# Linear attention and a sine MLP on one core: first hidden blocks by batch pairs, first k through two queues, decay moved from q to x, order redrawn

## The chip, the cores and the metric

The kernel runs on one core of a Trainium2 chip. The metric is device time of one execution in microseconds (us); lower is better. Engines are named as in the profile: PE is TensorE (PEld its weight loads), DVE is VectorE, ACT is ScalarE, POOL is GpSimd, SP is SyncE.

## The reference

Attention with decay, block by block, then an MLP with a sine. B = 4 batches, H = 8 heads, S = 768, D = 64; 3072 tokens, d_model 512, d_ff 2048, all fp32.

```python
for b in range(nb):                                   # causal blocks of the sequence
    intra = einsum('bhic,bhjc->bhij', qb, kb) * Dmask # lam^(i-j) for i >= j, else 0
    intra = einsum('bhij,bhjd->bhid', intra, vb)
    inter = einsum('bhid,bhde->bhie', qb * lam_pow, kv_state)   # lam^(i+1)
    out[:, :, sl] = intra + inter
    kv_state = lam_block * kv_state + einsum('bhsd,bhse->bhde', kb * rev_pow, vb)
x = out.transpose(0, 2, 1, 3).reshape(B * S, H * D)
h = x @ w_in
g = h + sin(alpha * h) ** 2 / (alpha + 1e-09)
y = g @ w_out
```

## The kernel before

The sequence is cut into six blocks t of T = 128 positions; a group g = t is that block of all four batches, 512 tokens. For each t the kernel forms scores transposed (`scores`, L241: k turned times q turned, heads in four row groups of 32, 32 products of 128 columns for a pair pr of batches), multiplies them on VectorE by a table of decays (`mask`, L253), adds the part that comes from the carried state (`carried`, L288) and the part inside the block (`inside`, L298) in four PSUM banks, one for each a (two heads), and casts them to xt in bf16 (`leave`, L312, a copy on ScalarE). The state is updated by `states` and `new_state` (L266, L277). The table C0 of t > 0 holds only the factor of k; the factor of q, lam^(i+1), is multiplied into the raw q on GpSimd by `scale_raw` (L261, word z) before `turn` (L232) transposes it on VectorE.

For each group the MLP has 16 blocks f of 128 hidden units: `hidden` (L321, four products of 512 columns), `sine` (L327, ScalarE), `square` (L331: on ScalarE for q, on VectorE as scalar_tensor_tensor for P, as tensor_tensor for Q), and `finish` (L341, VectorE, s^2 * r + h into gall). Then `project` (L347) multiplies gall by w_out in four parts of four f for each of four batches m, and `store` (L355) copies the result on ScalarE and sends it from SP. The last one goes in halves (L361).

PSUM has eight banks, which scores, outputs, states, hidden blocks and projections share; a word that needs a bank waits until its last reader is done. Each engine takes its instructions in the order in which the program issues them. From L498 that order is the ORDER table: a word is a step with its indices and, behind the colon, its banks. h, s, q/P/Q, t, u, o, e are the MLP as above; F, m, K, S, O, x are scores, masks, state products, new state, outputs, casts to xt; j and k turn q and k; d multiplies k by its decay on GpSimd (L257); B and C cast the state on ScalarE and GpSimd; r, R, n, v, I, W issue the loads of raw k, raw q, k, v, w_in, w_out from GpSimd's queue, which cast fp32 to bf16 on the way. Such a load waits for the eighth one before it.

The first block, t = 0, is written out ahead of the table (L148 to L460). SP loads k of two batches in fp32 (L150), which VectorE casts (L412); GpSimd loads the other pair (L160). ScalarE makes lnlam (L198) and the masks' table C1 (`decays`, L215), which GpSimd cuts to its triangle (`cut`, L219). k is turned on TensorE (`turn_k0`, L377), q on VectorE. Then follow scores and masks for each pair of batches, the products inside the block (`inside0`, L390) and the casts to xt (`leave0`, L400); `spin` (L182) issues products of ones whose result nobody reads. The last things ahead of ORDER are a `warm` sine on ScalarE (L458), which brings the table of sines, the reciprocal of alpha (L459) and C0 (L224). ORDER begins with h0.0.

Of the kernel before, what the change touches and what calls it, by code (L numbers as in the profile page):

```python
# [8 lines left out]
ALU = mybir.AluOpType  # L9
# [19 lines left out]
m2.1.3 B1.1 B2.0 m2.1.2 u1.1.3 o1.1 z3.0 v3 m2.1.1 z3.1 k3.0 o1.0 u1.2.1 O2:3275 x2.0 x2.1 x2.2 u1.2.2 x2.3 j3.0
F3.0:6043 m3.0.0 u1.2.3 o1.2 h2.0:6 m3.0.2 s2.0 q2.0 m3.0.1 j3.1 h2.1:7 s2.1 q2.1 k3.1 d3.1 h2.5:5 t2.0 R4  # L30
# [27 lines left out]
def kernel(  # L58
# [90 lines left out]
    for b in range(2):  # L149
        nc.sync.dma_start(out=raw_k0[:, b], in_=k[b, :, 0:T, :].rearrange("h p e -> p h e"))  # L150
# [161 lines left out]
    def leave(t, a):  # L312
        A.copy(out=xt[t][:, a, :].rearrange("p (b i) -> p b i", b=B), in_=att["O"][a])  # L313
# [217 lines left out]
```

## Time and profile before

| | us |
|---|---|
| median of 3 runs | 210.99 |
| the runs | 209.92, 210.99, 212.38 |
| profiled execution, its time | 209.95 |
| profiled execution, its span (first to last instruction) | 208.2 |
| busy in it: PE, DVE, ACT, POOL | 194.9, 145.8, 136.2, 100.7 |
| casts to xt on ACT (L313), 20 | 10.4 |
| raw q times decay on POOL (L263), 10 | 19.1 |
| squares on ACT (L335) 64, DVE P (L339) 19, DVE Q (L337) 13 | 39.2, 15.1, 5.5 |

The span counts from the first instruction to the last; the execution's own time has 1.75 us more. Each engine's instructions are dated in us from the start of the span. A product's record covers its pipeline, so that records of one stream overlap; the distance between starts is what one costs. What an engine waited for stands in brackets behind the first instruction after the wait.

### The profile page before, as it was taken

The numbers are of one execution on the slowest core, as the hardware profiler recorded it, in microseconds if no ns is written. First come the engines' busy times: TensorE is split into PE (matmuls) and PEld (weight loads), VectorE is DVE, ScalarE is ACT, GpSimd is POOL, SyncE is SP. The second block draws the span as 40 slices with busy tenths as digits, with TensorE's granted clock in tenths as the row PEclk, the third lists the DMA queues.
The fourth block names the chain that finished last, engine by engine and source line by source line (L and its number), as shares of the span: only waits on it lengthen the run. The fifth ranks groups of instructions, "written<-read, shape, count | busy, mean of one in ns | idle before, by whom it ended". The sixth has DMA issues, their size and how long they took to land.

```text
span 208.2 us, 4876 instructions
## 1 busy us (share of the span) xinstructions
PE 194.9 (94%) x2005; PEld 97.7 (47%) x2032; DVE 145.8 (70%) x218; ACT 136.2 (65%) x241; POOL 100.7 (48%) x116
## 2 busy tenths in 40 slices
PE   6479999999999999899999999999999999999993
PEld 3353444464444454354544564454444444444462
DVE  3486799742999879998897798774637876754300
ACT  4767999027999857948977577965626765455131
POOL 8999847979999986995717380000000000000000
DMA  7999999999995999999709969100111011011042
GB/s 132 166 181 180 187 200 207 170 175 232 213 140 58 153 173 186 122 119 168 49 3 122 180 85 74 50 3 3 50 50 50 0 50 54 0 52 50 4 153 98
DMA packets 65880, 22.61 MB, mean 109 GB/s; under 512 B 46770, under 2 KB 62914, under 8 KB 65858
## 3 DMA queue, kind: packets, MB, share of 16 engines
q0 software_dynamic: 60144, 15.47, 77.1%
q1 hardware_dynamic: 5680, 6.82, 9.4%
q8 instruction: 16, 0.26, 0.5%
q14 instruction: 6, 0.05, 0.1%
q10 hardware_dynamic: 34, 0.01, 0.0%
HBM read 31.47 MB, written 6.29 MB: 181 GB/s over the span
## 4 chain that ended last, share of the span: by engine, by line
PE 67%; POOL 12%; DMA 10%; DVE 4%; issue 4%; ACT 2%; POOLq 0%; DVEq 0%; ACTq 0%
PE ops L351 30%; PE hps L324 28%; DMA w_in<-in_moe_w_in_dram 4%; DMA raw_k<-in_k_dram 3%; DMA nat_v<-in_v_dram 3%; POOL w_in L141 3%; PE F_ps L248 2%; PE O_ps L303 2%; POOL raw_q L263 2%; POOL raw_q L124 2%; POOL nat_v L131 2%; PE ops L366 2%; DVE STm L254 1%; DVE s L339 1%; PE O_ps L294 1%
## 5 line engine op out<-in xcount | busy, mean ns | idle before, releaser
L324 PE MATMUL hps<-xt,w_in 128*128 128x512 bf16 x371 | 89.6, 383 | 1.0 <-issue 0.4
L351 PE MATMUL ops<-w_out,gall 128*128 128x512 bf16 x354 | 84.3, 379 | 1.6 <-issue 1.3
L329 ACT ACTIVATE s_sb<-hps,alpha_sb 128x512 bf16<-128x512 f32 x96 | 63.4, 690 | 27.9 <-PE hps L324 26.1
L344 DVE SCALAR_TENSOR_TENSOR gall<-s,r_sb,hps 128x512 bf16<-128x512 bf16 x96 | 67.7, 737 | 9.2 <-ACT s L335 8.2
L324 PEld LDWEIGHTS <-w_in 128*128 128x128 bf16 x384 | 37.3, 99 | 45.3 <-issue 2.1
L351 PEld LDWEIGHTS <-gall 128*128 128x128 bf16 x368 | 35.0, 98 | 41.7
L335 ACT ACTIVATE s<-s_sb 128x512 bf16<-128x512 bf16 x64 | 39.2, 636 | 1.0
L254 DVE TENSOR_TENSOR STm<-F_ps,C 128x512 bf16<-128x512 f32 x48 | 30.1, 682 | 6.5 <-PE F_ps L248 6.4
L357 ACT COPY o_sb<-ops 128x512 f32<-128x512 f32 x23 | 13.2, 585 | 26.6 <-PE ops L351 25.1
L259 POOL TENSOR_TENSOR nat_k<-nat_k,R 128x1024 bf16<-128x1024 bf16 x10 | 19.1, 1914 | 5.5 <-DMA nat_k<-in_k_dram 5.4
L263 POOL TENSOR_TENSOR raw_q<-raw_q,Rraw 128x1024 bf16<-128x1024 bf16 x10 | 19.1, 1919 | 4.8 <-DMA raw_q<-in_q_dram 4.8
L339 DVE SCALAR_TENSOR_TENSOR s<-s_sb 128x512 bf16<-128x512 bf16 x19 | 15.1, 804 | 7.4 <-ACT s_sb L329 7.2
L238 DVE STREAM_TRANSPOSE turned_q<-raw_q 128x512 f32<-128x512 f32 x12 | 13.0, 1096 | 7.5 <-POOL raw_q L263 5.2
L124 POOL DMA_DIRECT2D raw_q<-in_q_dram x24 | 14.2, 602 | 2.4 <-DVE turned_q L238 1.1
L124 POOL DMA_DIRECT2D raw_k<-in_k_dram x20 | 11.7, 602 | 5.5 <-DVE turned_k L238 4.6
L131 POOL DMA_DIRECT2D nat_v<-in_v_dram x12 | 14.2, 1186 | 0.0
L248 PE MATMUL F_ps<-turned_q,turned_k 32*128 32x128 bf16 x384 | 8.9, 229 | 5.2 <-DVE turned_q L238 2.8
L313 ACT CAST xt<-O_ps 128x512 bf16<-128x512 f32 x20 | 10.4, 596 | 4.7 <-PE O_ps L303 4.6
L337 DVE TENSOR_TENSOR s<-s_sb 128x512 bf16<-128x512 bf16 x13 | 5.5, 423 | 10.7 <-ACT s_sb L329 10.7
L238 DVE STREAM_TRANSPOSE turned_k<-raw_k 128x512 f32<-128x512 f32 x10 | 11.0, 1095 | 1.8 <-DMA raw_k<-in_k_dram 1.8
L248 PEld LDWEIGHTS <-turned_k 32*128 32x128 bf16 x384 | 6.5, 99 | 10.3 <-issue 6.4
L131 POOL DMA_DIRECT2D nat_k<-in_k_dram x9 | 10.7, 1192 | 0.1
(59 smaller groups left out, 86.8 us busy)
## 6 DMA issues: line engine op xcount, KB each, us to landing
out_dram<-o_sb SPq DMA_DIRECT2D x23, 256.0 KB, 2.3
raw_q<-in_q_dram POOLq DMA_DIRECT2D x24, 128.0 KB, 4.6
nat_v<-in_v_dram POOLq DMA_DIRECT2D x12, 256.0 KB, 6.4
raw_k<-in_k_dram POOLq DMA_DIRECT2D x20, 128.0 KB, 5.4
nat_k<-in_k_dram POOLq DMA_DIRECT2D x9, 256.0 KB, 8.5
w_out<-in_moe_w_out_dram POOLq DMA_DIRECT2D x4, 512.0 KB, 10.0
w_in<-in_moe_w_in_dram POOLq DMA_DIRECT2D x6, 256.0 KB, 7.1
raw_k<-in_k_dram SPq DMA_DIRECT2D x2, 256.0 KB, 3.6
```

The source lines that it names most:

```text
L124: (eng or G).dma_start(out=dst[quad[a], bs].rearrange("t b n r d -> t (b n) (r d)"), in_=src[t, a])
L131: G.dma_start(out=nat[nm, t][:, bs].rearrange("p b h e -> p (b h) e"), in_=SRC[nm][bs, :, t * T:(t + 1) * T, :].rearrange("b h p e -> p (b ...
L238: V.transpose(out=dst.rearrange("p (x t r) -> p x r t", r=R, t=32), in_=src.rearrange("p (x r d) -> p x r d", r=R, d=32))
L248: nc.tensor.matmul(out=F[a][:, u, n, :], lhsT=kt[:, :, e] if t else kt[:, e, :], rhs=KQ["q", t][quad[a], 2 * pr + u, n, :, e], start=(e == ...
L254: V.tensor_tensor(out=st[t, pr][:, a], in0=att["F", pr][a], in1=(C0 if t else C1)[:, a].unsqueeze(1).broadcast_to([P, 2, NQ, T]), op=ALU.mult)
L259: G.tensor_tensor(out=kd, in0=kd, in1=R128[:].unsqueeze(1).unsqueeze(3).broadcast_to([P, 2, H, D]), op=ALU.mult)
L263: G.tensor_tensor(out=qs, in0=qs, in1=Rraw[:].rearrange("p n r -> p (n r)").unsqueeze(1).unsqueeze(3).broadcast_to([P, 2, NQ * R, D]), op= ...
L324: nc.tensor.matmul(out=hps[g, f][:], lhsT=w_in_sb[f // 4][:, c, (f % 4) * P:(f % 4 + 1) * P], rhs=xt[g][:, c, :], start=(c == 0), stop=(c ...
L329: A.activation(out=s_of[g, f][:], in_=hps[g, f][:], func=ACTF.Sin, scale=alpha_sb[:, f:f + 1])
L335: A.activation(out=s2_of[g, f][:], in_=s_sb[:], func=ACTF.Square)
L344: V.scalar_tensor_tensor(out=gall[g][:, f, :], in0=s2_of.pop((g, f))[:], scalar=r_sb[:, f:f + 1], in1=hps.pop((g, f))[:], op0=ALU.mult, op ...
L351: nc.tensor.matmul(out=ops[g, m][:], lhsT=gall[g][:, f, m * P:(m + 1) * P], rhs=w_out_sb[part][:, f % 4, :], start=(f == 0), stop=(f == NF ...
```

## The change

For t = 0: all four batches of k come in fp32, two from SP and two from ScalarE's queue (alpha's load stands between the latter), and VectorE casts four. GpSimd issues the loads of q first, then makes `dist`, then loads v and the first half of w_in's first quarter; the quarter's other half and the second quarter are issued between the cuts of C1. The hidden blocks f = 0 to 3 of group 0 leave ORDER: `hidden_half` multiplies them by the 256 columns of one pair of batches and one c at a time, between the products inside the block, with more `spin` products among them. Scores of both pairs are issued ahead of all `inside0`. For t > 0: q is no longer scaled (the words z, `scale_raw`, `Rraw` and `ptab` go), and xt gets the factor lam^(i+1) as it leaves PSUM, by a tensor_tensor with the table `Etab` on VectorE in place of the copy on ScalarE. `Etab` is made by four Exp on ScalarE just ahead of the `warm` sine, from `pos_row` and four more columns of lnlam, for which `lam_half` is turned by four more products.

ORDER is redrawn: 651 words for 666. It has the same steps but for the 10 z, the four h and one I (w_in's second quarter); squares are 60 q, 19 P, 17 Q (before 64, 19, 13). The diff, with the table cut to its start:

```diff
--- before.py
+++ after.py
@@ -14,43 +14,42 @@
 ORDER = """
-h0.0:1 s0.0 I1 h0.1:2 s0.1 P0.0 q0.1 t0.0 t0.1 I2 d0.1 h0.2:0 s0.2 h0.3:3 I3 s0.3 q0.2 q0.3 h0.4:6 t0.2 r1 t0.3
-d0.0 h0.5:1 s0.4 s0.5 h0.6:7 P0.4 h0.7:4 s0.6 s0.7 P0.5 t0.4 t0.5 W0 R1 h0.8:5 q0.6 t0.6 s0.8 q0.7 P0.8 W1
...
+s0.0 s0.1 d0.1 P0.0 P0.1 t0.0 t0.1 s0.2 q0.2 t0.2 s0.3 q0.3 t0.3 I2 h0.5:5 h0.4:4 s0.4 s0.5 h0.6:7 h0.7:0 P0.4
+t0.4 q0.5 t0.5 h0.8:2 s0.6 P0.6 t0.6 h0.11:1 h0.9:3 R1 j1.0 I3 s0.7 s0.8 q0.7 t0.7 s0.9 q0.8 t0.8 W0 h0.10:4
+h0.13:6 q0.9 h0.12:7 W1 t0.9 s0.10 h0.14:2 u0.2.0:0 s0.11 h0.15:3 r1 q0.10 P0.11 t0.11 s0.12 s0.13 q0.12 q0.13
+W2 t0.10 j1.1 u0.0.0:1 v1 d0.0 t0.12 s0.14 u0.3.0:4 u0.0.1 K0:57 W3 s0.15 q0.14 t0.13 t0.14 q0.15 t0.15 S0.0
+C0.0 u0.2.1 k1.0 u0.3.1 S0.1 k1.1 F1.0:3527 m1.0.0 m1.0.1 u0.0.2 C0.1 u0.3.2 m1.0.2 m1.0.3 F1.1:6532 m1.1.1
+m1.1.3 u0.1.0:7 u0.2.2 m1.1.2 u0.1.1 m1.1.0 O1:3625 x1.0 x1.3 x1.1 u0.2.3 o0.2 u0.3.3 o0.3 u0.0.3 o0.0 x1.2
+h1.0:5 s1.0 r2 k2.1 k2.0 R2 n1 n2 v2 q1.0 h1.1:1 s1.1 h1.3:3 t1.0 j2.0 q1.1 t1.1 h1.2:4 s1.2 q1.2 t1.2 h1.4:0
...
@@ -145,21 +144,27 @@
-    raw_k0 = gbp.tile([P, 2, H, D], FP32, name="raw_k0", tag="gall")
-    for b in range(2):
-        nc.sync.dma_start(out=raw_k0[:, b], in_=k[b, :, 0:T, :].rearrange("h p e -> p h e"))
+    raw_k0 = gbp.tile([P, B, H, D], FP32, name="raw_k0", tag="gall")
     alpha_fp = consts.tile([NFC, P], FP32, name="alpha_fp")
+
+    def load_k0(eng, b):
+        eng.dma_start(out=raw_k0[:, b], in_=k[b, :, 0:T, :].rearrange("h p e -> p h e"))
+
+    load_k0(nc.sync, 0)
+    load_k0(A, 1)
+    load_k0(nc.sync, 2)
     A.dma_start(out=alpha_fp[:], in_=moe_alpha.rearrange("(f p) -> f p", p=P))
-    dist = consts.tile([P, T], FP32, name="dist")
-    G.iota(out=dist[:], pattern=[[1, T]], base=0, channel_multiplier=-1, allow_small_or_imprecise_dtypes=True)
+    load_k0(A, 3)
     new_raw(0, "q")
     new_nat(0, "k")
     new_nat(0, "v")
     for a in range(NA):
         load_raw(0, "q", a)
-    load_nat(0, "k", 1)
+    dist = consts.tile([P, T], FP32, name="dist")
+    G.iota(out=dist[:], pattern=[[1, T]], base=0, channel_multiplier=-1, allow_small_or_imprecise_dtypes=True)
     load_nat(0, "v", 0)
     load_nat(0, "v", 1)
+    load_w_in(0, 2, 0)
     fill = consts.tile([P, 512], BF16, name="fill")
     V.memset(fill[:], 1.0)
     one = consts.tile([1, 1], FP32, name="one")
@@ -168,10 +173,6 @@
     delta = consts.tile([P, T], FP32, name="delta")
     tri = consts.tile([P, T], FP32, name="tri")
     idf = consts.tile([NFC, NFC], FP32, name="idf")
-    V.tensor_scalar(out=iden[:], in0=dist[:], scalar1=0.0, scalar2=None, op0=ALU.is_equal)
-    V.tensor_copy(out=idf[:], in_=iden[0:NFC, 0:NFC])
-    V.tensor_scalar(out=delta[:], in0=dist[:], scalar1=0.0, scalar2=None, op0=ALU.max)
-    V.tensor_scalar(out=tri[:], in0=dist[:], scalar1=0.0, scalar2=None, op0=ALU.is_ge)
     pcol = consts.tile([P, 2], FP32, name="pcol")
 
     def token_column(n, base, step):
@@ -185,8 +186,8 @@
             nc.tensor.matmul(out=ps[:], lhsT=fill[:, 0:P], rhs=fill[:], start=True, stop=True)
 
     spin(3, 3)
-    lnall = consts.tile([P, H + NQ], FP32, name="lnlam")
-    lnlam, ln_q = lnall[:, 0:H], lnall[:, H:H + NQ]
+    lnall = consts.tile([P, H + NQ + NA], FP32, name="lnlam")
+    lnlam, ln_q, ln_a = lnall[:, 0:H], lnall[:, H:H + NQ], lnall[:, H + NQ:]
     lam_ps = bank("lam_ps", 2)
     for h in range(H):
         nc.tensor.transpose(out=lam_ps[:, h:h + 1], in_=lam_row[:, h:h + 1].broadcast_to([1, P]), identity=one[:])
@@ -195,7 +196,16 @@
     for n in range(NQ):
         nc.tensor.transpose(out=lam_ps[:, H + n:H + n + 1], in_=lam_quad[:].rearrange("p h i -> p (h i)")[
             :, n * P:n * P + P], identity=one[:])
-    A.activation(out=lnall[:], in_=lam_ps[:, 0:H + NQ], func=ACTF.Ln)
+    lam_half = consts.tile([1, NA, NQ, D], FP32, name="lam_half")
+    V.tensor_copy(out=lam_half[:], in_=lam_row[:].rearrange("p (n a) -> p a n", a=NA).unsqueeze(3).broadcast_to([1, NA, NQ, D]))
+    V.tensor_scalar(out=iden[:], in0=dist[:], scalar1=0.0, scalar2=None, op0=ALU.is_equal)
+    V.tensor_copy(out=idf[:], in_=iden[0:NFC, 0:NFC])
+    V.tensor_scalar(out=delta[:], in0=dist[:], scalar1=0.0, scalar2=None, op0=ALU.max)
+    V.tensor_scalar(out=tri[:], in0=dist[:], scalar1=0.0, scalar2=None, op0=ALU.is_ge)
+    for a in range(NA):
+        nc.tensor.transpose(out=lam_ps[:, H + NQ + a:H + NQ + a + 1], in_=lam_half[:, a].rearrange("p n d -> p (n d)"),
+                            identity=one[:])
+    A.activation(out=lnall[:], in_=lam_ps[:, 0:H + NQ + NA], func=ACTF.Ln)
     a_ps = bank("a_ps", 5)
     nc.tensor.transpose(out=a_ps[:, 0:NFC], in_=alpha_fp[:], identity=idf[:])
     spin(2, 3)
@@ -204,8 +214,8 @@
     NE = consts.tile([P, H], FP32, name="NE")
     R128 = consts.tile([P, H], FP32, name="R128")
     L128 = consts.tile([P, NQ], FP32, name="L128")
-    Rraw = consts.tile([P, NQ, R], FP32, name="Rraw")
-    ptab = consts.tile([P, R], FP32, name="ptab")
+    Etab = consts.tile([P, NA, T], FP32, name="Etab")
+    pos_row = consts.tile([P, T], FP32, name="pos_row")
     alpha_sb = consts.tile([P, NFC], FP32, name="alpha_sb")
     r_sb = consts.tile([P, NFC], FP32, name="r_sb")
 
@@ -258,11 +268,6 @@
         kd = nat["k", t][:, 2 * pr:2 * pr + 2]
         G.tensor_tensor(out=kd, in0=kd, in1=R128[:].unsqueeze(1).unsqueeze(3).broadcast_to([P, 2, H, D]), op=ALU.mult)
 
-    def scale_raw(t, pr):
-        qs = raw["q", t][:, 2 * pr:2 * pr + 2].rearrange("p b n r d -> p b (n r) d")
-        G.tensor_tensor(out=qs, in0=qs, in1=Rraw[:].rearrange("p n r -> p (n r)").unsqueeze(1).unsqueeze(3).broadcast_to(
-            [P, 2, NQ * R, D]), op=ALU.mult)
-
     def states(t, bks):
         KV = [bank("KV_ps", n)[:].rearrange("p (b e d) -> p b e d", b=B, e=2) for n in bks]
         kd = nat["k", t][:].rearrange("p b h (d e) -> p b h d e", e=2)
@@ -310,7 +315,8 @@
         inside(t, 1)
 
     def leave(t, a):
-        A.copy(out=xt[t][:, a, :].rearrange("p (b i) -> p b i", b=B), in_=att["O"][a])
+        V.tensor_tensor(out=xt[t][:, a, :].rearrange("p (b i) -> p b i", b=B), in0=att["O"][a],
+                        in1=Etab[:, a].unsqueeze(1).broadcast_to([P, B, T]), op=ALU.mult)
 
     def new_xt(t):
         xt[t] = xtp.tile([P, NDC, GRP], BF16, name="xt")
@@ -405,55 +411,82 @@
         else:
             V.tensor_copy(out=x, in_=o)
 
+    FIRST = (3, 0, 1, 2)
+
+    def hidden_half(pr, *pieces):
+        cols = slice(2 * pr * T, 2 * pr * T + 2 * T)
+        for f, c in pieces:
+            if (0, f) not in hps:
+                hps[0, f] = bank("hps", FIRST[f])
+            nc.tensor.matmul(out=hps[0, f][:, cols], lhsT=w_in_sb[0][:, c, f * P:(f + 1) * P], rhs=xt[0][:, c, cols],
+                             start=(c == 0), stop=(c == NDC - 1), skip_group_check=True)
+
     new_xt(0)
-    decays(0)
-    decays(1)
-    for b in range(2):
+    for b in range(B):
         V.tensor_copy(out=nat["k", 0][:, b], in_=raw_k0[:, b])
     turn(0, "q", 0)
     turn(0, "q", 1)
+    decays(0)
     turn_k0((0,), 4, A)
     turn_k0((1,), 7, A)
+    decays(1)
+    A.copy(out=alpha_sb[:], in_=a_ps[:, 0:NFC])
+    turn_k0((2,), 6, A)
+    turn_k0((3,), 5, A)
     decays(2)
     decays(3)
-    A.copy(out=alpha_sb[:], in_=a_ps[:, 0:NFC])
     cut(0)
     cut(1)
-    load_w_in(0, 2, 0)
+    load_w_in(0, 2, 1)
+    load_w_in(1)
     cut(2)
     cut(3)
-    load_w_in(0, 2, 1)
     token_column(0, -1, -1)
     token_column(1, T - 1, -1)
-    for a in range(NA):
-        G.iota(out=ptab[quad[a]], pattern=[[1, R]], base=1, channel_multiplier=R, allow_small_or_imprecise_dtypes=True)
+    G.iota(out=pos_row[:], pattern=[[1, T]], base=1, channel_multiplier=0, allow_small_or_imprecise_dtypes=True)
+    spin(2, 3)
     scores(0, 0, (0, 1, 2, 3))
-    turn_k0((2, 3), 6, A)
-    for a in range(NA):
-        mask(0, 0, a)
+    spin(1, 4)
+    scores(0, 1, (4, 5, 6, 7))
+    for pr in range(2):
+        for a in range(NA):
+            mask(0, pr, a)
     power(NE, 0)
     power(R128, 1)
+
+    spin(2, 0)
+    ps = open0(0)
+    inside0(0, 0, ps, 0, True)
+    spin(1, 1)
+    inside0(0, 1, ps, 1, False)
+    leave0(0, 0, 2, ps, A)
+    spin(1, 1)
+    ps = open0(1)
+    inside0(0, 2, ps, 0, True)
+    leave0(0, 2, 1, ps, A)
     A.activation(out=L128[:], in_=ln_q, func=ACTF.Exp, scale=float(T))
-    for n in range(NQ):
-        A.activation(out=Rraw[:, n, :], in_=ptab[:], func=ACTF.Exp, scale=ln_q[:, n:n + 1])
-    scores(0, 1, (4, 5, 6, 7))
-    for j in range(2):
-        ps = open0(j)
-        for a in (2 * j, 2 * j + 1):
-            inside0(0, a, ps, a % 2, a % 2 == 0)
-        leave0(0, 2 * j, 2, ps, A)
+    hidden_half(0, (1, 0), (1, 1))
+    ps = open0(2)
+    inside0(0, 3, ps, 0, True)
+    leave0(0, 3, 1, ps, A)
+    hidden_half(0, (0, 0), (0, 1), (0, 2), (1, 2))
+    late = [open0(4), open0(5), open0(6)]
+    inside0(1, 0, late[0], 0, True)
+    hidden_half(0, (0, 3), (1, 3))
+    inside0(1, 1, late[0], 1, False)
+    leave0(1, 0, 2, late[0], A)
+    hidden_half(0, (2, 0), (2, 1), (2, 2), (2, 3))
+    inside0(1, 2, late[1], 0, True)
+    leave0(1, 2, 1, late[1], A)
+    hidden_half(0, (3, 0), (3, 1), (3, 2), (3, 3))
+    hidden_half(1, (0, 0), (0, 1))
+    inside0(1, 3, late[2], 0, True)
+    leave0(1, 3, 1, late[2], V)
+    hidden_half(1, *((f, c) for f in (1, 2, 3) for c in (0, 1)))
+    hidden_half(1, *((f, 2) for f in range(4)))
+    hidden_half(1, *((f, 3) for f in range(4)))
     for a in range(NA):
-        mask(0, 1, a)
-    ps = open0(2)
-    inside0(1, 0, ps, 0, True)
-    inside0(1, 1, ps, 1, False)
-    leave0(1, 0, 2, ps, A)
-    ps = open0(3)
-    inside0(1, 2, ps, 0, True)
-    leave0(1, 2, 1, ps, A)
-    ps = open0(4)
-    inside0(1, 3, ps, 0, True)
-    leave0(1, 3, 1, ps, V)
+        A.activation(out=Etab[:, a, :], in_=pos_row[:], func=ACTF.Exp, scale=ln_a[:, a:a + 1])
     warm = consts.tile([P, 1], FP32, name="warm")
     A.activation(out=warm[:], in_=lnlam[:, 0:1], func=ACTF.Sin)
     V.reciprocal(out=r_sb[:], in_=alpha_sb[:])
@@ -486,7 +519,7 @@
 
     STEP = {
         "I": load_w_in, "W": load_w_out, "r": lambda t: load_raws(t, "k"), "R": lambda t: load_raws(t, "q"),
-        "v": lambda t: load_nats(t, "v"), "n": lambda t: load_nats(t, "k"), "z": scale_raw, "d": decay_k,
+        "v": lambda t: load_nats(t, "v"), "n": lambda t: load_nats(t, "k"), "d": decay_k,
         "k": lambda t, pr: turn(t, "k", pr), "j": lambda t, pr: turn(t, "q", pr), "F": scores_of, "m": mask,
         "K": states_of, "S": new_state, "O": outputs_of, "x": leave_x,
         "B": lambda t, n: cast_state(t, n, A), "C": lambda t, n: cast_state(t, n, G),
```

64 lines of the change are left out of this document (29 added, 35 removed).

## Prediction

> **What bounds the kernel now.** Four views, in this order: busy times by stage, the timeline of the first 20 us, TensorE's weight loads there, TensorE's waits from 60 to 110 us.
>
> ```profile
> 16.00:26.00 10.00, 9.78 (x42) 4.25 (x43) 7.15 (x12) 8.65 (x16) 9.00 (x13) 1.00 1.24 183
> 36.00:46.00 10.00, 9.79 (x176) 5.02 (x178) 6.96 (x11) 1.07 (x2) 8.89 (x13) 1.00 1.61 172
> 86.00:96.00 10.00, 8.63 (x128) 4.28 (x129) 9.78 (x15) 6.65 (x12) 9.99 (x10) 1.00 1.38 127
> ```
> Columns: stretch, length, busy PE, PEld, DVE, ACT, POOL, clock, DMA. From 16 us on PE is nearly always busy; it lacks 1.37 us at 86-96, where DVE is full. The head, and those holes, are all there is to win.
>
> ```profile
> 8.04 2.02 DVE L238 STREAM_TRANSPOSE turned_q<-raw_q 128x512 f32<-128x512 f32 x2 [2.33 <-DMA raw_q<-in_q_dram]
> 9.20 1.04 PE L248 MATMUL F_ps<-turned_q,turned_k 32*128 32x128 bf16 x32 [2.78 <-DVE turned_q L238]
> 10.31 2.48 DVE L254 TENSOR_TENSOR STm<-F_ps,C 128x512 bf16<-128x512 f32 x4 [0.25 <-PE F_ps L248]
> 13.38 2.48 DVE L254 TENSOR_TENSOR STm<-F_ps,C 128x512 bf16<-128x512 f32 x4 [0.58 <-PE F_ps L248]
> 16.17 1.28 ACT L458 ACT_TABLE_LOAD   x1
> 18.25 0.69 ACT L329 ACTIVATE s_sb<-hps,alpha_sb 128x512 bf16<-128x512 f32 x1 [0.59 <-PE hps L324]
> ```
> The head is a chain: q lands (8.04), scores, eight masks (end 15.86), xt, ACT's table of sines, the first hidden block and first sine (18.25).
>
> ```profile
> 16.67 0.15 PEld L324 LDWEIGHTS <-w_in 128*128 128x128 bf16 x1 [0.28 <-issue]
> 17.10 0.15 PEld L324 LDWEIGHTS <-w_in 128*128 128x128 bf16 x1 [0.28 <-issue]
> ...
> 19.23 3.77 PEld L324 LDWEIGHTS <-w_in 128*128 128x128 bf16 x18 [0.27 <-issue]
> ```
> Until 19.23 a 512-column product takes 0.427 us, afterwards 0.216 (four in 0.863 in the chain), though the clock column says 1.00 throughout: the first seven hidden products lose 7 x 0.211 = 1.5 us.
>
> ```profile
> PE F_ps L248 <- DVE gall L344: 0.7, 1, 0.7
> PE F_ps L248 <- DVE STm L254: 0.4, 1, 0.4
> ```
> PE's two holes there wait for VectorE.
>
> **The head, step by step.**
> *Loads.* The SWDGE load of k's second pair (1.29 us of POOL) becomes two on SP and ACT (about 0.5 us each; ACT's come before its first table load, which moves from 1.74 to 2.7; what waits for it, lam_ps, moves from 4.14 to 4.85 with four more transposes of 0.17). POOL issues q some 0.5 us earlier, and iota after it: delta is ready at 4.5, before the first Exp. The two k loads of before land 1.25 us apart (casts at 4.04 and 5.29); two more cost q's landing between 0 and 2 x 1.25 = 2.5 us. I take 1.6: 0.52 MB at the 246 GB/s of 2-4 us is 2.1, less the 0.5. Four casts (0.43) stand ahead of the turn on VectorE and wait for k; I take k's last at 9.0, so they end with q. Turns at 9.6 (8.0 to 10.5). v keeps its date (issued at 5.2 and 6.4, 5.5 to 7.3 to landing), since k's SWDGE load is gone from before it; it is needed at 14.3. w_in0's first half is issued ahead of the cuts now, needed at 16.
> The Trainium skill, "DMA: Bandwidth & Descriptors", "Issuing engines are not separate DMA queues", says that transfers from all issuers share the same engines, so a second queue saves issue time alone; by it the 1.6 holds, without it 0, and the scores would start at 10.3 (next step).
> *Alpha* now stands behind a k load on ACT's queue, so a_ps and what PE holds behind it (turns of k) start near 6.9 instead of 5.36. Then the copies of k turned and two more Exp on ACT (0.52, 0.32 each) end at 9.5, the last turn of k may use alpha's bank (10.05), and two dummies (0.43 each) give 10.9; from q it is 9.6+1.05. First scores 10.9 (9.20 before).
> *Masks.* First one 1.1 later, 12.0; eight at 0.62 without the old gap end at 16.9 (15.86), the seventh at 16.3. POOL's cuts 2 and 3, now behind w_in1's issues, which wait for q, end near 13.1, before the third mask needs them (13.2). pcol follows; NE and R128 wait for it on ACT with the xt copies queued behind, but those need nothing before 15.4.
> *PE between.* Second scores end 13.45. Before the last ScalarE copy stand 4 dummies (0.43), 7 groups of inside0 (0.26) and 12 half products (0.21): 6.1 us at the low rate, 3.1 at the high, plus 0.6 of waits for xt: 17.1 to 20.2. The rate should rise midway: 18.0. The copy (0.37) ends at 18.4. The rest of the 32 half products (0.11 each, from the row of 256 columns, 32 in 3.51) ends near 20.
> *ACT.* New behind the copies: four Exp for Etab, 1.28; then table 1.28 and warm 0.20. First sine at **21.2** instead of 18.25. Bounds: 19.4 (q at 8.0, masks alone) to 23.4 (low rate throughout).
>
> So PE is ahead by some 1.0 us at 20.2, then runs out of banks: three further blocks (to 22.8), and the fourth takes the bank of f=1, free only after P, P, t, t on VectorE (24.6).
>
> **Group 0.** From the first sine VectorE has no rest: 16 t x 0.68, 5 P x 0.645, 4 turns x 1.01, 8 masks x 0.62 = 23.1. It starts 0.72 after the sine; then O1 (1.35 + 0.2 latency), four xt. These move from ACT (four in 2.05) to VectorE: price bounded by the cast from PSUM (0.423 for 256 columns, so 0.85) and by the mask, same shapes, 2.48/4 = 0.62: I take the mask. 21.2+0.7+23.1+1.55+2.5 = 49.1, and 0.2 for the wait of F1.1 on a mask: h1.0 at **49.3**. Before: 49.23, but with all 16 parts of u0 done; now two (1.73 us) are left. ACT's 27 activations at 0.56 (20.36 to 35.98 holds 28) end near 36.4, just under VectorE.
>
> **After 49.3.** By the ORDER words: 80 h and 78 u at 0.863 = 136.4; K 4 x 0.78, F 8 x 0.6, O 4 x 1.9, the last halves 3.5 = 19.0. Sum 155.4. Before: 76 u, 153.6, from 49.23 to PE's end at 204.97, so 2.1 of holes; 1.36 of them waits on turns, gall and masks (0.31 at 53.16, 0.68 and 0.37 at 87.9 and 88.5).
> - z goes: 10 x 1.92 of POOL and the 5.2 us that turned_q waited for it. It buys the 0.31 at most. Next late is raw_k1, now behind w_out1: about 35, needed at 38.
> - Sixteen later xt: 16 x 0.62 = 9.9 more on VectorE. From h1.0 to h4.0: 48 t, 27 masks, 15 turns, 8 S (0.70), 12 xt, 4 P, 6 Q (0.42) = 32.6+16.7+15.2+5.6+7.4+2.6+2.5 = 82.6 us, of 88.9 for PE's 49 h, 39 u, 4 K, 7 F, 3 O. It fits with 6 us to spare; before it was 76.1 of 85.2.
> - ScalarE loses the 16 casts and three squares: its o, s and q queue less, and no wait of PE stands behind it. VectorE's four more Q (0.42) are in groups with room.
> - The half products cost PE 32 x 0.11 = 3.5 for 16 x 0.216 = 3.5: nothing. Seven dummies stand where two stood, all while PE waits anyway for masks.
> I keep 0.7 of the holes and half of the 1.36: 1.4. PE ends at 49.3+155.4+1.4 = 206.1, against 204.97: **+1.1 us**. The profiled execution is 209.95 (span 208.2 and 1.75 around it), so 211.05; it lies 1.04 below the median 210.99. Part of that distance may be the moment at which the rate doubles, which matters less in the new head: I add 0.7 and forecast **211.8**.
>
> **Rivals.**
> 1. *VectorE becomes the bound* (slower): a tenth more work in 49-150 us. For it: 86-96, where 9.78 of 10 cost PE 1.37. Against: z and ACT's queue stop delaying it. Price: two more such stretches, 2 x 1.37 = 2.7: 214.5. Decides when VectorE passes 9.7 in 10 over two stretches. Chance 0.16.
> 2. *The rate stays low through the half products* (slower): before, PE was busy from 12.31 to 16.3 with short gaps and still slow until 19.23. Then the copy ends at 20.6, the sine at 23.4, 2.2 later: 214.0. Against: dummies and scores leave no gap from 9.5 on. Chance 0.14.
> The Trainium skill, "TensorE: Matmul & The Clock Gate", Part 1, has the full clock follow some 3.4 us of sustained work, in a window that runs free of the kernel. By it the rate rises between 13 and 17; the trace's 19.23 agrees for work dense from 15.9 only.
> 3. *The head is early* (faster): q unhurt, sine at 19.4, h1.0 at 47.5, holes 0.7: 47.5+155.4+0.7 = 203.6, 1.4 less than before: 208.6, without the 0.7, since the rate rises early here. To count as faster it has to keep the sine before 19.7. For it: loads from three queues may overlap better than the 1.25 us row. Chance 0.18.
> 4. *Nothing shows*: h1.0 comes 1.1 us sooner, because VectorE's 23.1 starts when the halves end near 20, with the table load hidden: PE then ends as before, 211.0. Against: Etab and the load stand behind the last copy on one queue. Chance 0.12.
>
> **How the numbers follow.** Forecast 0.40, nearly all within 1% of 210.99 (208.9 to 213.1; 1% is about what the runs, 209.92 to 212.38, can tell from no change), 0.04 of it above. Within: 0.36+0.12 = 0.48; slower 0.04+0.16+0.14 = 0.34; faster 0.18. The range takes in rivals 1 to 3 nearly whole: 208.4 to 214.8; the forecast's own is 210.3 to 213.2.
>
> **What would show it.** First q turn near 9.6, scores 10.9, masks in one row of eight, first sine near 21.2 with Etab and the table load before it; PE idle 22.8 to 24.6; VectorE over 9.5 in 10 from 22 to 45; no raw_q L263; h1.0 near 49.3; the xt row near 0.65. Wrong if the sine comes before 20 or after 22.5, if PE's holes after 50 exceed 3 us, or if the xt row is 0.85.

## The result, and the profile after

The changed kernel takes 213.74 us (median of 6 runs, 212.97 to 220.26) against 211.06 for the kernel before beside it (6 runs, 209.92 to 212.38): ratio 1.0118, 95% interval 1.0075 to 1.0161. One of the six, 220.26, ran at a granted clock of 0.992 (0.998 to 1.000 in the others) and is left out of the ratio. The changed kernel is slower by 1.2%. The forecast was 211.8, so 1.9 us too low; the time lies inside the range of 208.4 to 214.8.

The profiled execution of the changed kernel took 212.97 (span 211.2). Its dates beside the forecast's, all from the timelines:

| us from the span's start | before | forecast | after |
|---|---|---|---|
| first turn of q | 8.04 | 9.6 | 10.80 |
| first scores | 9.20 | 10.9 | 12.59 |
| last of the first masks ends | 15.86 | 16.9 | 18.62 |
| first sine | 18.25 | 21.2 | 23.41 |
| h1.0 | 49.23 | 49.3 | 51.64 |
| PE's end | 204.97 | 206.1 | 208.07 |
| from first sine to h1.0 | 30.98 | 28.1 | 28.23 |
| from h1.0 to PE's end | 155.74 | 156.8 | 156.43 |

The last two rows are differences of the ones above. Read from the bottom: the two long stretches took what the forecast said, to 0.4 us. The head alone came out wrong, by 2.2 us at the first sine, and that is carried to the end.

The timeline of the changed kernel (start, duration, engine, line, operation, count; in brackets the engine's idle time before it, and what ended that):

```profile
7.38 0.43 DVE L426 CAST nat_k<-raw_k 128x512 bf16<-128x512 f32 x1 [0.59 <-DMA raw_k<-in_k_dram]
...
10.46 0.43 DVE L426 CAST nat_k<-raw_k 128x512 bf16<-128x512 f32 x1 [2.65 <-DMA raw_k<-in_k_dram]
10.80 2.02 DVE L248 STREAM_TRANSPOSE turned_q<-raw_q 128x512 f32<-128x512 f32 x2
...
12.59 1.13 PE L258 MATMUL F_ps<-turned_q,turned_k 32*128 32x128 bf16 x32
13.75 4.87 DVE L264 TENSOR_TENSOR STm<-F_ps,C 128x512 bf16<-128x512 f32 x8 [0.93 <-PE F_ps L258]
...
17.70 0.38 PE L421 MATMUL hps<-xt,w_in 128*128 128x256 bf16 x2
...
18.24 0.61 PE L421 MATMUL hps<-xt,w_in 128*128 128x256 bf16 x4
...
20.46 0.37 ACT L410 CAST xt<-O_ps 128x256 bf16<-128x256 f32 x1 [0.19 <-PE O_ps L399]
20.73 1.27 ACT L489 ACTIVATE Etab<-pos_row,lnlam 128x128 f32<-128x128 f32 x4
...
22.00 1.28 ACT L491 ACT_TABLE_LOAD   x1
...
23.41 1.82 ACT L335 ACTIVATE s_sb<-hps,alpha_sb 128x512 bf16<-128x512 f32 x3
...
26.77 1.02 PE L330 MATMUL hps<-xt,w_in 128*128 128x512 bf16 x4 [1.14 <-DVE gall L350]
...
48.81 2.48 DVE L318 TENSOR_TENSOR xt<-O_ps,Etab 128x512 bf16<-128x512 f32 x4 [1.66 <-PE O_ps L308]
```

The chain is the forecast's, with each link late. VectorE waits 2.65 us for the fourth batch of k, and only then turns q; scores, eight masks in one row (4.87, so 0.61 each), the last ScalarE copy, Etab, table of sines, first sine. The half products of 256 columns run at 0.11 us each from 17.70 on (two in 0.38, four in 0.61, so 0.23 for two more): the high rate came early. At 26.77 is the bank wait that was forecast (1.14 us for 1.8), and the four xt cost 0.62 each, as forecast.

That VectorE waits for k here does not mean that q was there. The times of q's four loads from issue to landing, before and after (the last one was issued at 3.37 and at 3.31):

```profile
DMA to landing us min/median/max: 4.3/4.5/4.6
```

```profile
DMA to landing us min/median/max: 6.1/6.7/7.1
```

So q's last load landed at 7.9 before and at 10.4 after, almost together with k's last. Before, k's second pair was the last to land, 5.7 us after its issue at 3.93, thus at 9.7. In the changed kernel k's last was cast at 10.46. All of k and q together came 0.8 us later, and q is no longer through ahead of the rest.

The windows of the changed kernel, for the same stretches as before (length, busy PE, PEld, DVE, ACT, POOL, clock, DMA):

```profile
16.00:26.00 10.00, 9.52 (x79) 5.48 (x79) 6.17 (x12) 7.51 (x17) 9.19 (x14) 1.00 1.13 166
36.00:46.00 10.00, 10.00 (x166) 4.85 (x164) 9.86 (x15) 3.94 (x8) 4.17 (x8) 1.00 1.62 176
86.00:96.00 10.00, 10.00 (x138) 4.79 (x136) 9.36 (x16) 9.26 (x17) 5.37 (x8) 1.00 1.56 172
```

PE's hole at 86-96 is gone, and after h1.0 PE waits only once, 0.79 us at 76.2, for nothing that the profile shows.

### The profile page after: what moved, and what is told of

Read it like the earlier page. It is cut to its first block, busy times and chain, and to the rows that moved or that the text cites. A ratio compares the mean times of both kernels' runs of the same rounds, so it can differ in the third digit from the quotient of the medians.

```text
span 211.2 us, 4968 instructions
## 1 busy us (share of the span) xinstructions
PE 199.7 (95%) x2059; PEld 99.4 (47%) x2059; DVE 159.0 (75%) x245; ACT 125.9 (60%) x221; POOL 80.3 (38%) x102
## 4 chain that ended last, share of the span: by engine, by line
PE 87%; DVE 4%; DMA 3%; ACT 2%; issue 2%; ACTq 0%; DVEq 0%
PE ops L357 38%; PE hps L330 34%; PE F_ps L258 4%; DMA alpha_fp<-in_moe_alpha_dram 3%; PE O_ps L308 2%; DVE gall L350 2%; PE spare L186 2%; PE ops L372 2%; PE O_ps L299 2%; PE KV_ps L278 1%; DVE s L345 1%; PE hps L421 1%; PE O_ps L399 1%; ACT Etab L489 1%; DVE turned_q L248 1%
## 5 line engine op out<-in xcount | busy, mean ns | idle before, releaser
L330 PE MATMUL hps<-xt,w_in 128*128 128x512 bf16 x368 | 87.0, 379 | 1.7 <-DVE gall L350 1.7
L357 PE MATMUL ops<-w_out,gall 128*128 128x512 bf16 x368 | 87.7, 379 | 0.0
L350 DVE SCALAR_TENSOR_TENSOR gall<-s,r_sb,hps 128x512 bf16<-128x512 bf16 x96 | 68.4, 737 | 9.6 <-ACT s L341 8.4
L330 PEld LDWEIGHTS <-w_in 128*128 128x128 bf16 x368 | 35.4, 98 | 44.4 <-issue 2.6
L341 ACT ACTIVATE s<-s_sb 128x512 bf16<-128x512 bf16 x60 | 36.7, 633 | 0.9
L264 DVE TENSOR_TENSOR STm<-F_ps,C 128x512 bf16<-128x512 f32 x48 | 30.2, 683 | 4.9 <-PE F_ps L258 4.7
L318 DVE TENSOR_TENSOR xt<-O_ps,Etab 128x512 bf16<-128x512 f32 x20 | 12.7, 683 | 4.0 <-PE O_ps L308 3.9
L345 DVE SCALAR_TENSOR_TENSOR s<-s_sb 128x512 bf16<-128x512 bf16 x19 | 13.1, 696 | 2.7 <-ACT s_sb L335 2.7
L123 POOL DMA_DIRECT2D raw_k<-in_k_dram x20 | 11.6, 589 | 1.8 <-DVE STm L264 1.5
L343 DVE TENSOR_TENSOR s<-s_sb 128x512 bf16<-128x512 bf16 x17 | 7.0, 418 | 4.6 <-ACT s_sb L335 4.4
L130 POOL DMA_DIRECT2D nat_k<-in_k_dram x8 | 9.3, 1170 | 0.3 <-PE ops L357 0.3
L186 PE MATMUL spare<-fill 128*128 128x512 bf16 x12 | 5.8, 565 | 1.5 <-DVE one L171 1.5
```

What stands on the lines that cost most here:

```text
L123: (eng or G).dma_start(out=dst[quad[a], bs].rearrange("t b n r d -> t (b n) (r d)"), in_=src[t, a])
L130: G.dma_start(out=nat[nm, t][:, bs].rearrange("p b h e -> p (b h) e"), in_=SRC[nm][bs, :, t * T:(t + 1) * T, :].rearrange("b h p e -> p (b ...
L264: V.tensor_tensor(out=st[t, pr][:, a], in0=att["F", pr][a], in1=(C0 if t else C1)[:, a].unsqueeze(1).broadcast_to([P, 2, NQ, T]), op=ALU.mult)
L330: nc.tensor.matmul(out=hps[g, f][:], lhsT=w_in_sb[f // 4][:, c, (f % 4) * P:(f % 4 + 1) * P], rhs=xt[g][:, c, :], start=(c == 0), stop=(c ...
L341: A.activation(out=s2_of[g, f][:], in_=s_sb[:], func=ACTF.Square)
L345: V.scalar_tensor_tensor(out=s2_of[g, f][:], in0=s_sb[:], scalar=1.0, in1=s_sb[:], op0=ALU.mult, op1=ALU.mult)
```

## The experiments

Twelve kernels. "Theory" stands for: the loss lies in the head, because nothing of attention starts before all of k and q has landed. Ratios are against the kernel before, run beside each.

### The head of before, the rest of the change

The head, k's loads and the whole hidden blocks of before; xt times Etab on VectorE, no scaling of q, and the new ORDER with its own start:

```
-s0.0 s0.1 d0.1 P0.0 ...
+h0.0:3 s0.0 I1 h0.1:0 h0.2:1 h0.3:2 s0.1 d0.1 P0.0 ...
```

> The head of before (k by SP and GpSimd, hidden blocks 0 to 3 whole, no extra dummies) with the rest of the change: q unscaled, xt times Etab on VectorE, the new ORDER, which gets h0.0 to h0.3 and the load of w_in's second quarter back at its start; the four Exp of Etab stand where Rraw's stood. Theory (the loss sits wholly in the head): first sine near 18.5 instead of 23.4, h1.0 near 47.5 instead of 51.8, PE's end near 203.5, time 208 to 209, faster than before. Rival (VectorE's new work or the new ORDER costs the time): h1.0 near 49 or holes of over 3 us after it, 212 to 214.

Measured: 218.82 median of 4 (214.58, 218.61, 219.04, 219.97), and no ratio, since they lie so far apart; the profile is of 218.61. A miss, and no verdict on the theory: the first sine came at 18.74, but in that execution two other things took the gain. A square on VectorE lasted 3.29 us instead of 0.69, which cost PE 1.90 at 35.5. And in O2 PE stood for 4.52 us, after which the products took 0.43 us again until 85.7. The window:

```profile
76.00:86.00 10.00, 5.14 (x20) 1.98 (x16) 5.61 (x8) 0.59 (x1) 4.54 (x4) 0.66 0.63 64
```

Both are taken up below.

### The later part of the change alone

The kernel before with q unscaled and xt times Etab on VectorE, in the old ORDER without its z words.

> The kernel before with the move of the decay alone: no z, xt times Etab on VectorE, Etab in Rraw's place, ORDER of before without its z. Theory (the move is about neutral: it frees GpSimd and turned_q, and VectorE has room): 209.5 to 211.5. Rival (VectorE becomes the bound): PE's holes from 50 to 150 us grow by 3 us or more, 213 to 215.

Measured: 219.44 median of 4, ratio 1.0389 (1.0321 to 1.0457). My theory, that this part is neutral by itself, fell. PE's waits in it (us in all, times, longest):

```profile
PE hps L289 <- DVE xt L277: 2.9, 3, 1.5
...
PE F_ps L217 <- DVE turned_q L207: 2.3, 1, 2.3
...
PE hps L289 <- DVE gall L309: 1.7, 1, 1.7
```

The h blocks that follow an x word in the old table now wait for VectorE's queue, where ScalarE made xt before. Behind the 2.3 us for turned_q the seven next products of 512 columns took 0.43 us each, 1.5 us more than at 0.216, and the clock column (last but two) shows it:

```profile
80.00:84.00 4.00, 4.00 (x41) 1.71 (x42) 3.22 (x5) 0.59 (x1) 0.03 (x1) 0.57 0.02 2
```

With the redrawn table and the old head the same move of the decay comes out level (0.9998 below, with two further edits). The redrawn table is a needed part of the change, not an ornament to it.

### Etab's four Exp ahead of the xt copies

```
     power(R128, 1)
+    for a in range(NA):
+        A.activation(out=Etab[:, a, :], ...)
```

> The changed kernel with the four Exp of Etab moved from behind the last xt copy to behind NE and R128, into the 1.7 us in which ScalarE waits for inside0. Theory (ScalarE's chain of copy, Etab, table load, first sine is the path): first sine 1.2 earlier, 22.2, and all after it; 212.5. Rival (the path runs over PE or the loads, the sine waits anyway): no shift, 213.7.

Measured: 213.38 median of 10, ratio 1.0095 (1.0059 to 1.0131). That is 0.4 us under the changed kernel's median, and the intervals overlap, so no gain is shown. The first sine is still at 23.44, now with `[0.47 <-PE hps L421]`: it waits for PE's half products. In this execution they began at 18.32 instead of 17.70, since the high rate came later (the two dummies at 15.32 took 1.03 us together, 0.81 in the changed kernel). In the changed kernel they end at 22.88, so there some 0.5 of the 1.28 us of Etab would be on the path, by my estimate.

### k's second pair through GpSimd, as before

```
-    load_k0(A, 1)
-    load_k0(nc.sync, 2)
+    load_k0(nc.sync, 1)
...
-    load_k0(A, 3)
+    load_nat(0, "k", 1)
```

> The changed kernel with the loads of k as before: two batches by SP, the other pair cast by GpSimd's queue behind q; alpha alone on ScalarE's queue. Theory (the fp32 loads beside q and alpha behind them make the scores late): alpha's product near 4.5 instead of 7.8, q turned from about 9 instead of 10.8, scores near 11.3 instead of 12.6, first sine about 1.2 earlier, 212.5. Rival (all loads share the same engines, so it does not matter who issues k): scores at 12.6 and 213.7.

Measured: 213.59 median of 4, ratio 1.0103 (1.0027 to 1.0178), the rival's time; but the head did what the theory said. From its timeline:

```profile
8.22 2.00 DVE L247 STREAM_TRANSPOSE turned_q<-raw_q 128x512 f32<-128x512 f32 x2 [1.52 <-DMA raw_q<-in_q_dram]
...
10.03 1.03 PE L388 MATMUL T_ps<-iden,nat_k 128*128 128x128 bf16 x8 [2.64 <-DMA nat_k<-in_k_dram]
11.85 1.13 PE L257 MATMUL F_ps<-turned_q,turned_k 32*128 32x128 bf16 x32
...
32.95 1.80 DVE L344 SCALAR_TENSOR_TENSOR s<-s_sb 128x512 bf16<-128x512 bf16 x1
```

q is back at 8.2, the first sine at 22.12, 1.3 earlier. It could not be more, because the scores still wait for the turns of k's second pair (10.03); and a square of 1.80 us on VectorE gives 1.1 of it back, so h1.0 is at 51.01, 0.6 earlier.

### alpha's load first

The load of alpha issued ahead of both k loads on ScalarE's queue.

> The changed kernel with alpha's load issued ahead of both k loads on ScalarE's queue. Theory (the head ends with the last landing of k, alpha only holds the turns of k's first pair, which have time): a_ps moves from 7.76 to 4.5 to 5.5, the first pair's turns with it, but scores stay at 12.2 to 12.7, first sine at 23.0 to 23.5, the time within 0.4 of 213.7. Rival (alpha holds the head): scores at 11.6, first sine at 22.4, the time 212.7.

Measured: 213.74 median of 4, ratio 1.0129 (1.0076 to 1.0182). As the theory said: a_ps at 5.42 instead of 7.76, scores at 12.64, first sine at 23.07, no gain.

### K2 later

```
-K2:20 B1.0 B1.1 O2:6435 ... o1.0 u1.2.1 h2.0:4
+B1.0 B1.1 O2:6435 ... o1.0 u1.2.1 K2:20 h2.0:4
```

> The changed kernel with one word of ORDER moved: K2 (64 weight loads and 64 matmuls of the state sums) stands ahead of h2.0 instead of directly ahead of O2, so the 320 PE instructions that ran there in 2.4 us are spread. Theory: the 0.79 us in which PE waited for nothing the profile shows, at 76 us in the middle of O2, is PE waiting for its own instructions (a fetch of 16 KB came 2.3 us before it ended), because short matmuls use them up faster than they are fetched. Then the hole goes or shrinks below 0.3, and the median falls by 0.5 to 0.8, to 213.0. Rival: the hole belongs to that fetch and comes wherever PE is at that moment, whatever runs there: the hole stays at 0.8 and the median at 213.7.

Measured: 212.73 median of 4, ratio 1.0105 (1.0069 to 1.0141), and the hole is gone, as the theory said. The medians lie 1.0 us apart, but the intervals of the ratios overlap, so that the hole's 0.79 us is shown by the trace and not by the times. In this execution the four casts ran at 5.42, 6.40, 8.21 and 11.29, and q was later still:

```profile
12.02 2.03 DVE L248 STREAM_TRANSPOSE turned_q<-raw_q 128x512 f32<-128x512 f32 x2 [0.30 <-DMA raw_q<-in_q_dram]
```

So q itself can land near 12 with four loads of k beside it, 4.0 us after its date before; in the changed kernel's own profile it was 2.5.

### The head of before once more, without the two accidents

As the first experiment, with K2 later and block 11's square in group 0 on ScalarE (`q0.11` for `P0.11`).

> The head of the kernel before with the rest of the change (decay moved to x, new ORDER with a short start of its own), as in the first such run, but with K2 moved ahead of h2.0 and square P0.11 given to ScalarE (q0.11), so that neither the 4.5 us hole in O2 nor the square that took 3.3 us on VectorE should come back. Theory (the loss lies in the new head alone): first sine 18.7, h1.0 near 49, PE's end at 49 + 155.4 + 1.5 = 206, the time 207.8, to 209.5 at most, below the kernel before. Rival (the new order and VectorE's sixteen xt cost at least as much as the head): holes of over 4 us after 50 us, 212 or more.

Measured: 210.92 median of 10, ratio 0.9998 (0.9977 to 1.0020): level with the kernel before, where the theory had it below. First sine 18.82, h1.0 49.65, PE's end 206.43, as summed (206). PE stood 1.01 us for nothing shown just ahead of h1.0, and 0.79 in K2; both come up again at the end. The time that I put beside it (207.8) left out the 3.2 us between PE's end and the span's; with the 5.0 from PE's end to the time that the kernel before has, 206 is 211.0. So the later part and its table, with K2 moved, are worth just what they replace, and the new head costs the rest: 212.73 with K2 later against 210.92, 1.8 us (the two also differ in block 11's square, which was not lengthened in either).

### Three mends together

The changed kernel with k's second pair through GpSimd, Etab early, K2 later.

> Three of the mends together on the changed kernel: k's second pair through GpSimd as before, Etab's four Exp moved ahead of the xt copies, K2 moved ahead of h2.0. Theory (the head's lateness and the hole in O2 are all that was lost): first sine 21.6 to 22.1 instead of 23.4, no hole in O2, the time 211.5 to 212.2. Rival (what the head gains is given back to VectorE, which is the bound in group 0, or to a later wait): first sine as said, h1.0 no earlier than 51.3, the time 213 or more.

Measured: 212.94 median of 4, ratio 1.0100 (1.0060 to 1.0139). First sine 22.18, no hole in O2, yet h1.0 at 51.56: the rival's numbers. VectorE and GpSimd in its timeline:

```profile
32.82 1.91 POOL L268 TENSOR_TENSOR nat_k<-nat_k,R 128x1024 bf16<-128x1024 bf16 x1
33.02 2.27 DVE L344 SCALAR_TENSOR_TENSOR s<-s_sb 128x512 bf16<-128x512 bf16 x1
```

The earlier head moved block 11's square onto GpSimd's product of k: 1.6 us lost. The product ends at 34.73, the square 0.56 later.

### Scores of the first pair ahead of the turns of the second, and the squares exchanged

```
+    scores(0, 0, (0, 1, 2, 3))
     turn_k0((2,), 6, A)
     turn_k0((3,), 5, A)
...
-... P0.11 ... q0.15 ...
+... q0.11 ... P0.15 ...
```

> The kernel with the three mends (k's second pair through GpSimd, Etab early, K2 later), and two more: the first pair's scores stand ahead of the turns of k's second pair on PE, as before the change, and in group 0 the squares of blocks 11 and 15 change engines (q0.11, P0.15), so that none runs on VectorE beside GpSimd's product of k. Theory (the new head's price is that no score starts before all four batches of k are turned): first scores at 10.6 instead of 12.23, first sine 20.4 to 21.0 instead of 22.18, no square over 0.75, h1.0 48.7 to 49.5, PE's end 204.5 to 205.5, the time 209.5 to 210.5. Rival (PE's rate rises later when the first scores come alone, so the head keeps its length): first sine 21.8 or later, 211.5 or more.

Measured: 210.92 median of 12, ratio 0.9980 (0.9949 to 1.0010). First scores 9.71, first sine 21.16, no square over 0.75, h1.0 50.09, PE's end 205.95: the theory's direction, 0.2 to 0.6 us short. The third mask waited 0.49 for GpSimd's cut, and the sine 0.47 for the half products. With five edits the changed kernel is level with the one before. The five were not taken apart, so what each is worth in time is not shown.

### The old head with VectorE and ScalarE evened out

As "The head of before once more", with `P0.15` for `q0.15`.

> The head of before with the rest of the change and K2 later, the square of block 15 in group 0 now on VectorE (P0.15 for q0.15). ScalarE was late by 1.2 and 0.3 us for VectorE there, since it had 0.11's square in addition. Theory (then VectorE and ScalarE are even again, and the new order is worth as much as the old one or a little more): h1.0 at 49.0 to 49.4 instead of 49.65, PE's end 205.8 to 206.3, the time 210.2 to 210.8. PE's end lies 5.0 us before the time in the profiled execution of before (204.97 and 209.95), which the expectation for the kernel without this edit left out in part. Rival (the 1.0 us in which PE waited for nothing shown, at 48.4, comes back wherever VectorE and ScalarE stand): h1.0 and the time as without the edit, 210.9.

Measured: 211.45 median of 12, beside 211.74 for the kernel before in the same session, ratio 0.9991 (0.9961 to 1.0021): no change shown. In the profiled execution k's second batch was cast at 7.32 and q turned at 9.40 (8.04 before), so the first sine is at 19.60; from there to h1.0 it took 30.2 instead of 30.8. The 0.6 us came in that stretch, lost again to the later q, and lies below what these runs can show. h1.0 was at 49.80, outside the theory's range and next to the rival's 49.65; but the 1.0 us at 48.4 did not come back, so the rival's reason fell too.

### One square of the kernel before on ScalarE

```
-h2.2:1 t2.1 h2.3:2 d3.0 s2.2 s2.3 P2.2 t2.2
+h2.2:1 t2.1 h2.3:2 d3.0 s2.2 s2.3 q2.2 t2.2
```

> The kernel before with one letter of ORDER changed: the square of block 2 in group 2 on ScalarE (q2.2 for P2.2). On VectorE it took 2.90 us beside GpSimd's product of k, and ended 0.57 after that product did. Theory (VectorE's operation with two inputs in SBUF waits for GpSimd's, and PE's holes of 0.68 and 0.37 at 87.9 and 88.5 are its price): no square over 0.75 us, the two holes gone, the time 0.8 to 1.2 lower, 209.8. Rival (VectorE is full there anyway, as my prediction had it): holes of 0.6 or more stay between 86 and 96, and the time within 0.4 of 210.9.

Measured: 209.27 median of 11, ratio 0.9903 (0.9869 to 0.9936). One letter is worth 1%, and this version beats both kernels, the changed one with its five mends too (210.92 in the same session). The same place in the kernel before, and here:

```profile
83.52 2.90 DVE L339 SCALAR_TENSOR_TENSOR s<-s_sb 128x512 bf16<-128x512 bf16 x1
...
83.94 1.92 POOL L259 TENSOR_TENSOR nat_k<-nat_k,R 128x1024 bf16<-128x1024 bf16 x1
...
87.91 0.23 PE L248 MATMUL F_ps<-turned_q,turned_k 32*128 32x128 bf16 x2 [0.68 <-DVE gall L344]
...
88.51 0.61 PE L248 MATMUL F_ps<-turned_q,turned_k 32*128 32x128 bf16 x29 [0.37 <-DVE STm L254]
```

```profile
84.72 1.92 POOL L259 TENSOR_TENSOR nat_k<-nat_k,R 128x1024 bf16<-128x1024 bf16 x1
...
87.81 0.64 PE L248 MATMUL F_ps<-turned_q,turned_k 32*128 32x128 bf16 x32
```

The scores follow in one piece, with no wait. From h1.0 to PE's end it takes 154.20 (50.09 to 204.29) instead of 155.74. The two holes are 1.05 of these 1.54 us, and of the 2.1 us that the ratio gives; where the rest comes from is not shown.

### The new head without its dummies

The seven dummy products around the first scores and att-v products left out (they feed nothing).

> The changed kernel without the seven dummy products of its new head (two ahead of the first scores, one ahead of the second, four ahead of the first products of att and v). Theory (they bring the early rise of PE's rate, at 15.3): without them the half products run at 0.21 each until 18 to 20, first sine at 24.2 to 25.2 instead of 23.4, the time 214.5 to 215.5. Rival (scores and turns alone keep the rate, and the dummies cost PE 0.4 us each on the path): first sine 22.6 to 23.2, the time 213.0 to 213.5.

Measured: 215.98 median of 4, ratio 1.0161 (1.0075 to 1.0248). The half products ran low until about 20:

```profile
17.20 1.03 PE L421 MATMUL hps<-xt,w_in 128*128 128x256 bf16 x4
...
20.47 0.83 PE L421 MATMUL hps<-xt,w_in 128*128 128x256 bf16 x6
```

Four in 1.03, then six in 0.83; with the dummies it was high from 15.7. So they do bring the rate. Yet the first sine is at 23.53, neither theory's: what the low rate costs, the earlier start of the scores and products gives. The longer time is elsewhere: a square of 1.96 us beside GpSimd's product, and 2.27 of hole in O2. The interval overlaps the changed kernel's (1.0075 to 1.0161), so that the dummies' worth in time is not shown.

## Why the prediction was right and wrong

- **Loads: the step that failed.** "two more cost q's landing between 0 and 2 x 1.25 = 2.5 us. I take 1.6 ... I take k's last at 9.0". q's last load landed 2.5 later in the changed kernel's profile, 2.9 to 3.1 later in three other kernels with these loads, and 4.0 later with K2 later (12.02, where it was itself waited for); k's last was cast at 10.46. So the spacing of two loads was near the least that two more cost, not the most. Through GpSimd (k's second pair behind q) q is at 8.2 to 8.7 in three runs. The Trainium skill, "DMA: Bandwidth & Descriptors", section "Issuing engines are not separate DMA queues", says that transfers from all issuers share the same engines: the direction agrees, the 1.6 that I took beside it was too small. What is shown is the order of landing: the bytes of k and q read are the same in both kernels, and in the changed kernel's profile all of them land only 0.8 us later, but q now lands with the last of k instead of ahead of it. Why the whole takes longer, and how much lies in the number of loads and how much in their place ahead of q, was not tried.
- **The path of the scores** was wrong with it. The sum had alpha's path last (10.9, and 10.65 by q), with k's fourth batch at 9.0 out of the way. That batch came last: cast at 10.46, its turn on PE at 11.22, scores at 12.59. With alpha early the scores were no sooner (12.64). The 10.3 that stands beside the skill's rule does not fit the sum either, since alpha's 10.9 holds without any delay of q.
- **From the scores to the sine.** PE was through with the second scores at 15.29 for 13.45, 1.8 late; from there to the end of the last copy on ScalarE it took 5.5 us for 4.95, another 0.6; ScalarE's 2.6 behind the copy were 0.2 less than summed. That makes the 2.2 us at the first sine.
- **alpha** was late as said, and more (7.76 against 6.9), and harmless: moving it brought no gain.
- **Masks, copies, Etab, table load, xt** had the right prices; the first sine reached the stated upper bound (23.4) by the loads, not by the low rate that the bound was made of; that the two figures meet is luck. Of Etab, which I put whole into the path, some 0.5 is there at most, and moving it showed no gain.
- **Rival 2** (rate stays low) was wrong: the rate rose at 15.7. The Trainium skill, "TensorE: Matmul & The Clock Gate", Part 1, had it between 13 and 17 by some 3.4 us of sustained work: the trace agrees here, at 15.7, with dummies from 11.6. In the six other kernels with these dummies it was high by 14.2 to 15.2 in four, and only by 17.6 and 18.1 in two (Etab early, K2 later), which is outside. Without them it rose near 20.
- **Group 0**: 23.1 us of VectorE and the bank holes held (28.23 against 28.1 from sine to h1.0).
- **After h1.0**: 155.4 of work and 1.4 of holes held as a sum (156.43), for a wrong reason in part. The holes were not VectorE's waits: 0.79 of the 1.0 us beyond the work was one in O2.
- **Rival 1** misread the row before. "86-96, where 9.78 of 10 cost PE 1.37" was not a full VectorE: it was one square of 2.90 us, as the one-letter run shows. VectorE at 9.73 in 136-146 of the changed kernel, and at 9.84 in 86-96 with K2 later, cost PE nothing (10.00 both times).
- **The chances.** Within 1% had 0.48; it came out at 1.2% slower. Neither slower rival is what happened; the forecast's own upper bound of the head is, and I gave it too little. The last 0.7, added for the distance between the profiled execution and the median, came out (0.77, 212.97 to 213.74), but its reason, the moment at which the rate doubles, was not tested, so that is luck as far as the runs show.

Where did the change's gain go? The first masks without a gap between the pairs, no scaling of q on GpSimd and no hole at 86-96 are real: PE is at 10.00 in nearly every window after h1.0. Behind the old head they come to nothing (0.9998): the new table leaves 1.73 us more of u work for after h1.0, and there PE took 156.8 (49.65 to 206.43) instead of 155.74. The new head then starts everything 2.4 us later than the kernel before.

## What to carry to other kernels

Before moving a load to another queue, look at who lands last for the first consumer, and at the order of the consumer's own queue: here q landed with the last of k instead of ahead of it, and one barrier (all of k) held every score. An engine at 98% in a window is not yet the bound: look at the longest single instruction in it against the median of its row, and at what runs beside it. A mend at one end of a schedule shifts what stands side by side at the other; three edits that each did their part left the ratio at 1.0100 (1.0118 without them), and the square that they pushed onto GpSimd's product took 1.6 us of the head's gain.

## What the runs showed of the hardware that was not expected

**Squares on VectorE wait for GpSimd's product.** The square (one SBUF tile read as both inputs) takes 0.68 to 0.69. Ten squares in nine kernels overlapped the product of k: each ended 0.54 to 0.57 after it, whether it began 0.8 us before the record of the product (3.29 long) or 0.2 before its end (0.75). GpSimd's product kept its 1.9 us. Squares that overlapped only GpSimd's DMA issues kept 0.68 to 0.70. `finish`, with one input in PSUM, kept 0.66 to 0.75 throughout. The Trainium skill, "SBUF — State Buffer", section "Who interferes with whom", says that a VectorE instruction with two inputs in SBUF contends with a GpSimd instruction that reads SBUF, and that the order of issue decides who blocks. The traces agree on the contention; two squares whose records start first waited all the same, but records on GpSimd are rough.

**PE stands at a fixed number of its instructions, probably for want of the next ones.** The changed kernel, and the one without dummies:

```profile
75.84 0.36 PE L308 MATMUL O_ps<-STm,nat_v 128*64 128x128 bf16 x6
77.00 0.92 PE L308 MATMUL O_ps<-STm,nat_v 128*64 128x128 bf16 x26 [0.79 <-issue]
```

```profile
76.78 0.58 PE L308 MATMUL O_ps<-STm,nat_v 128*64 128x128 bf16 x13
79.63 0.75 PE L308 MATMUL O_ps<-STm,nat_v 128*64 128x128 bf16 x19 [2.27 <-issue]
```

Seven products fewer ahead, and the hole stands seven products later (13 for 6). With the head of before, 23 fewer, it stood 23 later (29 for 6). With K2 moved on top of that, it stood in K2 itself, at the product where the same count falls:

```profile
77.88 0.53 PE L272 MATMUL KV_ps<-nat_v,nat_k 128*32 128x64 bf16 x45
79.20 0.33 PE L272 MATMUL KV_ps<-nat_v,nat_k 128*32 128x64 bf16 x19 [0.79 <-issue]
```

So the hole is tied to a number in PE's own stream. In the three kernels with the new head and K2 later the same number falls 22 products into K2, and no hole shows there: the place alone does not make one. The queue named instruction moves 16 pieces, 0.26 MB in all: worked out, 64 bytes for each of 2059 products and as many weight loads, 256 of them a piece. In all eight kernels with such a hole in O2 or K2 a piece began to move 2.4 to 2.9 us before PE went on, whether the hole lasted 0.34 us or 4.52. So its length (0.43, 0.79, 0.95, 1.77 and 2.27 in five kernels at the same number) goes with how late the piece moves. My reading: where K2 and O2 stand one behind the other, 320 instructions go in some 2.5 us and use a piece up before the next is there; 512-column products, at 0.216 us, mostly hide it. They do not always: the 1.01 us just ahead of h1.0 in the old head's second version stands among them, and there too a piece began to move 2.5 us before PE went on. Why a piece comes late was not tried.

**The rate can fall again after a hole.** In the first experiment, after 4.52 us, the products took 0.43 us for 4.3 us, with 0.66 in the clock column of that window. In the kernel with the later part alone it fell after a wait of 2.26 us, until 83.66 (0.57 from 80 to 84). After the 2.27 us in the kernel without dummies, and after the shorter holes in O2, the products kept 0.216. So the length of the hole alone does not decide it.
